# Subtractions of the first batch on VectorE, the first down-projection tile inside the up-projection, and fewer attention steps beside it

## The chip, the core and the metric

The kernel runs on one core of a Trainium2 chip. The metric is device microseconds of one execution; the time before is 673.47 us, the median of three runs (673.11 to 674.36).

## The reference, cut to what matters

Four batches of 576 positions go through windowed attention (8 heads of 64, window 64), a gated feed-forward layer, and a routed layer of eight experts.

```python
scores = scale * q @ k.T;  scores = where(0 <= rel < 64, scores, -1e9)
x = softmax(scores) @ v                                  # per batch and head, then heads side by side: 576 x 512
h = relu(x @ w_in)                                       # 512 -> 1024
conv_out = sum_k conv_w[k] * h shifted by k - 1          # three taps along the positions
y = (h * sigmoid(conv_out)) @ w_out                      # 1024 -> 512
e = argmax(y @ w_gate), held over from the position before where sigmoid(y @ w_local) >= 0.5
out = softmax(y @ w_gate)[e] * (relu(y @ w1[e]) @ w2[e])
```

## The kernel before, in words

**Numbers in two halves.** Matrix products run on float32 values split into a rounded high half H and a low half L, and each product is three: H times H, H times L, L times H. A split costs one ScalarE instruction (the rounding) and one subtraction. The feed-forward weights arrive as 64-bit floats and are first put together from two 32-bit words by three VectorE instructions (`bits64`, lines 558, 560, 562), then rounded by ScalarE and subtracted (`conv_chunk`, lines 583 and 584): `conv_in` does this for chunks of w_in (128 rows by 512 columns, eight in all), `conv_out` for the eight blocks of w_out. `conv_out` also transposes its block (line 602) and multiplies it with the gate weights (line 606), so that the routing logits come out of the down-projection as ten further columns.

**Stages.** The attention of batch 0 (`attention_first`) has nothing to run beside. It is written out by hand as the string `FIRST` of tokens, which sets the order of every engine there (the planner is off). After it, batch b's feed-forward part runs together with the attention of batch b+1: `mix` asks `main(b)` for one turn after the other (one turn per six accumulation steps) and, after each, takes as many of the 25 steps of `attention(b + 1)` as `share(b)` has allowed by then. In batch 0, 16 of the 25 steps are written beside the 32 turns of the up-projection and the rest beside the 16 turns of the four down-projection tiles. This program order gives the priorities; outside `FIRST` a planner puts each engine's instructions in order, and takes a later one first where an engine would otherwise stand still by its own reckoning. After batch 3 come the routing and the experts' tiles.

**The tokens of `FIRST`.** The digits are pair of heads (4 is the first pair of batch 1) and part. T: transposes of k, q and the tails on TensorE (lines 172 and 185), with k, q, t their evictions (q on ScalarE, line 196 for batch 1). S and R: scores on TensorE and their row maxima on VectorE (line 230). E: the exponentials (ScalarE, line 242, three of them). N and M: normalization on VectorE (N has lines 251 to 253 and the first product of line 255; M the other product). A and a: the probabilities transposed (line 270) and evicted by ScalarE. V, x, l: the product with v (line 298), its high half (ScalarE, line 305), its low half (VectorE, line 308). c, h, u: the three steps of a w_in chunk on VectorE, its rounding on ScalarE (line 650), its subtraction on GpSimd (line 652). D: matmuls of no use that keep TensorE busy (line 162). Z: a GpSimd memset and the loads of a pair of batch 1 on SP.

**Loads.** SP issues nearly all of them, in order. Before `FIRST`, pairs 0 to 3 of batch 0 and the first six chunks of w_in are asked for; the first two chunks stand between pairs, the other four in a row (line 571). The next pairs follow with Z0 and Z1.

**The up-projection** (`ffn`). For each of eight blocks f of 128 columns: two halves of twelve matmuls (line 432) into two banks, relu on ScalarE (line 439), the middle tap on ScalarE (451), two taps on VectorE (452, 453), tanh on ScalarE (454), the gate's product on VectorE (455), then gH by ScalarE (460) and gL (461) on GpSimd for all but the very last block. In batch 0 each block also starts one w_out block (and, for the first two, one of the last two w_in chunks), whose rounding, subtraction and transposes come one block later.

**The down-projection** (`ffn_out(i, fold)`). A tile of 128 positions takes 24 accumulation steps (eight blocks, three products each) into two banks at once (262 and 260 columns wide), so 48 matmuls (line 474), then two evictions and a store.

Of the kernel before, what the change touches and what calls it, by code (L numbers as in the profile page):

```python
# [21 lines left out]
def kernel(  # L22
# [70 lines left out]
    if True:  # L93
# [313 lines left out]
        def ffn(b):  # L407
            xs_b = xT.pop(b)
            fin = []
            t0 = b * S  # L410
            for f in range(KF):
                if b == B - 1 and f == 5:
                    gate(R0, I0)
                    gate_exp(0, I0)
                if b == 0:
                    if cin:
                        fin.append(conv_in(*cin.pop(0)))
                        if len(fin) > 1:
                            fin.pop(0)()
                    fin.append(conv_out(f))  # L420
                    if f:
                        fin.pop(0)()
                hbuf = hb[hcnt[0] % 2]
                hcnt[0] += 1
                for half in range(2):
                    ps = psm.tile([P, 512], F32, tag="m", name="psM")
                    c0 = half * HS
                    n = 0
                    for kk in range(KD):
                        xH, xL = xs_b[kk]  # L430
                        for wt, xt in ((winH, xH), (winH, xL), (winL, xH)):
                            nc.tensor.matmul(  # L432
                                ps[:, 0:HS], wt[:, kk, f * P:(f + 1) * P], xt[:, c0:c0 + HS],
                                start=n == 0, stop=n == 3 * KD - 1,
                            )
                            n += 1
                            if n == 6:
                                yield
                    nc.scalar.activation(hbuf[:, 1 + c0:1 + c0 + HS], ps[:, 0:HS], AF.Relu, scale=0.5)  # L439
                    yield  # L440
                t = tb[(b * KF + f) % 3]
                last = b == B - 1 and f == KF - 1
                cuts = (0, HS - 1, S) if last else (0, S)
                e1 = nc.vector if last else nc.gpsimd
                for u, w in zip(cuts, cuts[1:]):
                    tt = t[:, u:w]
                    h0, h1, h2 = (hbuf[:, j + u:j + w] for j in range(3))
                    if last:
                        nc.vector.tensor_scalar(tt, h1, cw[:, 1, f:f + 1], None, op0=ALU.mult)
                    else:  # L450
                        nc.scalar.activation(tt, h1, AF.Copy, scale=cw[:, 1, f:f + 1])
                    nc.vector.scalar_tensor_tensor(tt, h0, cw[:, 0, f:f + 1], tt, op0=ALU.mult, op1=ALU.add)  # L452
                    nc.vector.scalar_tensor_tensor(tt, h2, cw[:, 2, f:f + 1], tt, op0=ALU.mult, op1=ALU.add)
                    nc.scalar.activation(tt, tt, AF.Tanh)
                    nc.vector.scalar_tensor_tensor(tt, tt, 1.0, h1, op0=ALU.add, op1=ALU.mult)
                    done = u
                    while done < w:
                        r = (t0 + done) % RING
                        m = min(w - done, RING - r)
                        nc.scalar.activation(gH[:, f, r:r + m], t[:, done:done + m], AF.Copy)  # L460
                        e1.tensor_tensor(gL[:, f, r:r + m], t[:, done:done + m], gH[:, f, r:r + m].bitcast(F32), op=ALU.subtract)  # L461
                        done += m
            for x in fin:
                x()
# [122 lines left out]

        def conv_in(c, kk):
            fs = slice(c * CC, (c + 1) * CC)
            return conv_chunk(chunk_in(c, kk), winH[:, kk, fs], winL[:, kk, fs], nc.gpsimd, early.get((c, kk)))[1]  # L590

        def conv_out(kk):

            src = w_out.rearrange("(k p) f -> p k f", p=P)
            f, fin = conv_chunk(src[:, kk, :], woutH[:, kk, 0:DM], woutL[:, kk, 0:DM], nc.gpsimd)

            def finish():
                fin()
                wt = y_p.tile([P, KD, P], F32, tag="ysb", name="wt")
                pt = psa.tile([P, 512], F32, tag="a", name="psWT")  # L600
                for j in range(KD):
                    nc.tensor.transpose(pt[:, j * P:(j + 1) * P], f[:, j * P:(j + 1) * P], ident)
                nc.scalar.activation(wt.rearrange("p j f -> p (j f)"), pt, AF.Copy)
                ps = psa.tile([P, 512], F32, tag="a", name="psW")
                for j in range(KD):
                    nc.tensor.matmul(ps[:, 0:E1], wt[:, j, :], wgl[:, j, :], start=j == 0, stop=j == KD - 1)  # L606
                wH, wL = woutH[:, kk, DM:DW], woutL[:, kk, DM:DW]
                nc.scalar.activation(wH, ps[:, 0:E1], AF.Copy)
                nc.vector.tensor_tensor(wL, ps[:, 0:E1], wH.bitcast(F32), op=ALU.subtract)

            return finish
# [3 lines left out]
            S11 a00 R10 V00 R11 E10 A01 A02 S12 c00 x00 a01 l00 R12 a02 V01 c01 V02 x01 T20 x02 l01 E11 T21 l02 k2 T22  # L615
            t2 c02 q2 v2 E12 S20 S21 R20 N1 S22 E20 M1 A10 a10 R21 h0 V10 R22 A11 u0 x10 A12 a11 l10 Z0 T30 c10 a12
            V11 k3 E21 V12 c11 T31 T32 x11 t3 x12 l11 q3 l12 c12 E22 v3 S30 S31 R30 N2 S32 E30 M2 A20 a20 R31 h1 V20
            R32 A21 u1 x20 A22 a21 l20 T40 c20 a22 V21 k4 E31 V22 c21 T41 T42 x21 t4 x22 l21 q4 l22 c22 E32 c30 c31
            c32 h2 N3 h3 u2 M3 D9 A30 a30 u3 c40 V30 c41 A31 x30 A32 a31 l30 c42 a32 V31 c50 V32 x31 l31 x32 h4 l32
            c51 u4 c52 h5 u5 Z1  # L620
        """

        with tc.manual_schedule():
            warm(bank(0), 6)
            load_pair(0, 0)
            nc.vector.memset(wgl[:, :, E + 1:E1], 0.0)
            KC = 3 * KF
            taps = cv.tile([P, CC, 2], U32, tag="raw", name="cr", bufs=2)[0:KC, 0:P]
            nc.scalar.dma_start(out=taps.rearrange("r p t -> r (p t)"), in_=conv_w.rearrange("k (f x) -> (k f) x", f=KF))
            nc.scalar.dma_start(out=wgl[:, :, 0:E], in_=w_gate.rearrange("(k p) e -> p k e", p=P))  # L630
            nc.scalar.dma_start(out=wgl[:, :, E:E + 1], in_=w_local.rearrange("(k p) e -> p k e", p=P))
            cin = [(c, kk) for c in range(FF // CC) for kk in range(KD)]
            load_pair(0, 1)
            for i, (c, kk) in enumerate(cin[0:6]):
                early[c, kk] = load_chunk(st_p.tile([P, CC, 2], U32, name=f"raw{i}"), chunk_in(c, kk))
                if i < 2:
                    load_pair(0, 2 + i)
            part = {}

            def others(s_, i, g):  # L640

                c, kk = divmod(i, KD)
                fs = slice(c * CC, (c + 1) * CC)
                if s_ == "c":
                    if g == 0:
                        part[i] = cv.tile([P, CC], F32, name="lf")
                    bits64(early[c, kk], part[i], (g,))
                elif s_ == "h":
                    cin.pop(0)
                    nc.scalar.activation(winH[:, kk, fs], part[i], AF.Copy)  # L650
                elif s_ == "u":
                    nc.gpsimd.tensor_tensor(winL[:, kk, fs], part[i], winH[:, kk, fs].bitcast(F32), op=ALU.subtract)
                elif s_ == "w":
                    part["f"] = cv.tile([P, CC], F32, tag="lf", name="cf")[0:KC, 0:P]
                    bits64(taps, part["f"])
                elif s_ == "W":
                    part["ps"] = bank(0)
                    nc.tensor.transpose(part["ps"][:, 0:KC], part["f"], ident[0:KC, 0:KC])
                elif s_ == "Y":
                    nc.vector.tensor_copy(cw.rearrange("p k f -> p (k f)"), part["ps"][:, 0:KC])  # L660
                elif s_ == "D":
                    warm(bank(0), i)
                else:
                    nc.gpsimd.memset(qbds[i], 0.0)
                    load_pair(1, i)

            attention_first(FIRST, others)

# [243 lines left out]

        def share(b):

            n1, n2, na = 4 * KF, 4 * (4 + b % 2), 34 if b == 0 else 28
            return lambda m: 16 * m // n1 if m <= n1 else 16 + (na - 16) * (m - n1) // n2

        def main(b):
            yield from ffn(b)
            if b < B - 1:  # L920
                for i in range(b * S // P, (b + 1) * S // P):
                    yield from ffn_out(i, True)

        for b in range(B):
# [321 lines left out]
```

## Time and profile before

| | |
|---|---|
| median of three runs | 673.47 us |
| the profiled execution | 671.16 us |
| its span, first to last instruction | 669.4 us |
| TensorE busy, mean granted clock | 635.6 us (95%), 0.982 |
| VectorE busy | 500.5 us (75%) |
| ScalarE busy | 471.3 us (70%) |
| GpSimd busy | 151.5 us (23%) |

The profile is of one execution, so its parts add up to 671.16 and not to the median. Matmuls overlap in it, and their ends are modelled: a TensorE that is busy all the time can still be at half clock. The granted clock stands beside the busy time for that reason; 1.00 is 2.4 GHz and 0.50 is 1.2 GHz.

### The profile page before, as it was taken

To read this page: it belongs to the slowest core of one execution; us is meant where nothing else is said; L and a number is where in the kernel's file an instruction comes from. 1 tells how busy PE (TensorE), PEld (TensorE's weight loads), DVE (VectorE), ACT (ScalarE), POOL (GpSimd) and SP (SyncE) were. 2 spreads that over 40 slices of the span, in tenths; PEclk is the share of its full clock that TensorE was granted. 3 is DMA by queue.
4 is the path that set the end of the run, shared out by engine and by line. 5 is a ranking of instruction groups with operands and counts; after the bars stand their busy time and mean duration, and the time that the engine had idled before them with its cause. 6 is when DMAs were issued, how large, how long until landed. Compare 5 with 4: busy or idle time off the path is not lost.

```text
span 669.4 us, 12937 instructions
## 1 busy us (share of the span) xinstructions
PE 635.6 (95%) x4398; PEld 554.2 (83%) x4398; DVE 500.5 (75%) x989; ACT 471.3 (70%) x1003; POOL 151.5 (23%) x172
## 2 busy tenths in 40 slices
PE   6858898999999999999999999999999999999995
PEld 4647897899999999999978878888888888888884
DVE  4988987436884168725777788899899889889982
ACT  3855786536885478835625489888888988988982
POOL 2324625000330013303522221211211211211101
PEclk9989897899999999999999999999999999999998
DMA  8884414333234221108002147511451444512770
GB/s 166 214 214 108 130 46 117 77 95 95 64 69 104 64 52 33 32 33 315 1 0 79 48 174 256 194 48 52 153 164 64 145 157 157 166 41 71 240 273 14
DMA packets 91881, 75.77 MB, mean 113 GB/s; under 512 B 72266, under 2 KB 72290, under 8 KB 91812
## 3 DMA queue, kind: packets, MB, share of 16 engines
q1 hardware_dynamic: 85696, 63.78, 32.2%
q0 software_dynamic: 3680, 10.75, 4.8%
q10 hardware_dynamic: 2436, 0.37, 0.4%
q8 instruction: 36, 0.59, 0.4%
q14 instruction: 33, 0.27, 0.1%
HBM read 127.84 MB, written 11.27 MB: 208 GB/s over the span
## 4 chain that ended last, share of the span: by engine, by line
PE 41%; issue 32%; DMA 12%; DVE 6%; SPq 3%; POOL 2%; ACT 1%; ACTq 0%; POOLq 0%
PE psO L474 14%; PE psM L432 13%; DMA out_dram<-h,sidx 10%; PE psA L218 4%; PE psA L298 3%; PE psA L270 2%; PE psA L185 2%; POOL xg L1022 2%; PE psG L543 1%; DMA kt<-in_k_dram 1%; DVE lf L560 1%; PE psW L606 1%; DVE h L452 1%; PE psO L514 1%; SPq L141 1%
## 5 line engine op out<-in xcount | busy, mean ns | idle before, releaser
L432 PE MATMUL psM<-x,winH 128*128 128x288 f32 x512 | 111.0, 305 | 1.4 <-ACT h L439 1.3
L461 POOL TENSOR_TENSOR gL<-h,gH 128x576 fp32r<-128x576 f32 (+6 forms) x54 | 60.6, 1132 | 163.6 <-ACT gH L460 150.3
L432 PEld LDWEIGHTS psM<-x,winH 128*128 128x128 f32 x512 | 82.4, 189 | 3.7 <-ACT h L439 2.1
L1087 POOL DMA_INDIRECT out_dram<-h,sidx x23 | 23.3, 1014 | 233.4 <-ACT h L1086 233.4
L432 PE MATMUL psM<-x,winL 128*128 128x288 f32 x256 | 75.7, 296 | 0.0
L474 PE MATMUL psO<-woutH,gH 128*128 128x262 f32 (+2 forms) x240 | 68.8, 315 | 0.7 <-ACT gH L460 0.7
L474 PE MATMUL psO<-woutL,gH 128*128 128x262 f32 (+2 forms) x240 | 66.7, 306 | 1.2 <-POOL woutL L584 1.2
L1003 DVE TENSOR_TENSOR gL<-raw,gH 128x1024 fp32r<-128x1024 f32 x56 | 65.6, 1220 | 2.2 <-ACT gH L998 0.7
L474 PE MATMUL psO<-woutH,gL 128*128 128x262 f32 (+2 forms) x240 | 65.7, 304 | 0.0
L242 ACT ACTIVATE sS<-sS,mx 128x128 f32<-128x128 f32 (+1 forms) x144 | 55.2, 386 | 12.7 <-DVE mx L230 12.5
L1003 DVE TENSOR_TENSOR winL<-raw,winH 128x1024 fp32r<-128x1024 f32 x48 | 56.4, 1235 | 3.6 <-ACT winH L998 3.6
L998 ACT ACTIVATE gH<-raw 128x1024 fp32r<-128x1024 f32 x56 | 55.8, 1066 | 0.0
L1003 DVE TENSOR_TENSOR woutL<-raw,woutH 128x1024 fp32r<-128x1024 f32 x44 | 51.0, 1221 | 2.8 <-ACT woutH L998 2.8
L432 PEld LDWEIGHTS psM<-x,winL 128*128 128x128 f32 x256 | 48.2, 188 | 0.2
L998 ACT ACTIVATE winH<-raw 128x1024 fp32r<-128x1024 f32 x48 | 47.0, 1062 | 0.0
L1081 PE MATMUL psO<-x,hh 128*128 128x512 f32 x144 | 46.7, 404 | 0.0
L230 DVE CUSTOM_DVE_ANT_0 sS<-psA,mask 128x128 f32<-128x128 f32 (+1 forms) x135 | 31.0, 278 | 21.0 <-PE psA L218 16.8
L1003 DVE TENSOR_TENSOR x<-raw,x 128x1024 fp32r<-128x1024 f32 x36 | 42.0, 1220 | 5.2 <-ACT x L998 4.2
L474 PEld LDWEIGHTS psO<-woutL,gH 128*128 128x128 f32 x240 | 42.8, 190 | 3.2 <-POOL woutL L584 1.6
L474 PEld LDWEIGHTS psO<-woutH,gH 128*128 128x128 f32 x240 | 42.7, 190 | 2.7 <-ACT gH L460 0.9
L1081 PE MATMUL psO<-gH,hh 128*128 128x512 f32 x112 | 44.6, 398 | 0.0
L1081 PE MATMUL psO<-gH,hl 128*128 128x512 f32 x112 | 44.0, 393 | 0.0
(288 smaller groups left out, 1656.9 us busy)
## 6 DMA issues: line engine op xcount, KB each, us to landing
raw<-in_moe_w_dram SPq DMA_DIRECT2D x184, 512.0 KB
v<-in_v_dram SPq DMA_DIRECT2D x56, 128.0 KB
y_dram<-ysb SPq DMA_DIRECT2D x18, 256.0 KB
kt<-in_k_dram SPq DMA_DIRECT2D x32, 128.0 KB
raw<-in_moe_w_in_dram SPq DMA_DIRECT2D x8, 512.0 KB
raw<-in_moe_w_out_dram SPq DMA_DIRECT2D x8, 512.0 KB
qt<-in_q_dram SPq DMA_DIRECT2D x30, 128.0 KB
y_dram<-x SPq DMA_DIRECT2D x2, 256.0 KB
```

The source lines that it names most:

```text
L185: nc.tensor.transpose(ps[:, n * P:(n + 1) * P], src[:, n].rearrange("p h d -> p (h d)"), ident)
L218: nc.tensor.matmul(ps[:, j * P + lo:(j + 1) * P], qbd[:, c, :], kT[:, k0:W * (c + 1)], start=True, stop=True)
L230: nc.vector.tensor_tensor_reduce(sS[:, c, lo:P], ps[:, j * P + lo:(j + 1) * P], mask[:, lo:P], -scale, -NEG, op0=ALU.add, op1=ALU.min, acc ...
L242: nc.scalar.activation(sS[:, c, lo:P], sS[:, c, lo:P], AF.Exp, scale=-1.0, bias=mx[:, c:c + 1], accum_out=sume[:, c:c + 1],)
L298: nc.tensor.matmul(ps[64 * h:64 * h + 64, W * j:W * j + W], vt[:, h, :], a[0:kk, j, 64 * h:64 * h + 64], start=True, stop=True,)
L432: nc.tensor.matmul(ps[:, 0:HS], wt[:, kk, f * P:(f + 1) * P], xt[:, c0:c0 + HS], start=n == 0, stop=n == 3 * KD - 1,)
L461: e1.tensor_tensor(gL[:, f, r:r + m], t[:, done:done + m], gH[:, f, r:r + m].bitcast(F32), op=ALU.subtract)
L474: nc.tensor.matmul(p_[:, 0:cs.stop - cs.start], gt[:, kk, r:r + P], wt[:, kk, cs], start=n == 0, stop=n == 3 * KF - 1,)
L998: nc.scalar.activation(H_, raws[kk], AF.Copy)
L1003: nc.vector.tensor_tensor(L_, raws[kk], H_.bitcast(F32), op=ALU.subtract)
L1081: nc.tensor.matmul(ps, a[:, kk], w[:, kk % 2, :], start=n == 0, stop=n == 3 * KF - 1)
L1087: nc.gpsimd.indirect_dma_start(out=out[:, :], out_offset=bass.IndirectOffsetOnAxis(ap=sidx[:, t:t + 1].bitcast(U32), axis=0), in_=o, in_of ...
```

## The change

In batch 0 the subtractions of gL, of woutL and of the last two winL chunks are issued on VectorE instead of GpSimd. Tile 0 of the down-projection becomes a generator made before the loop (`out0`, a turn per three accumulation steps); from block 2 on, the first half of each block also takes one turn of it, so that six of its eight blocks are issued in the up-projection, two blocks behind. `share(0)` allows 12 steps of attention by the end of the up-projection and spreads the others, counted up to 29, over the 14 turns that are left. In `FIRST`, the last two pairs are put in another order: V21 and V22 ahead of T40, E31 behind x22, q4 behind E32, N3 and M3 ahead of chunk 3's first step (chunk 2 is then h2, chunk 3 h3), and D is 24 matmuls in three tokens instead of nine in one. Chunks 4 and 5 of w_in are loaded with Z0, behind the first pair of batch 1.

```diff
--- before.py
+++ after.py
@@ -437,11 +437,13 @@
                             if n == 6:
                                 yield
                     nc.scalar.activation(hbuf[:, 1 + c0:1 + c0 + HS], ps[:, 0:HS], AF.Relu, scale=0.5)
+                    if b == 0 and half == 0 and f > 1:
+                        next(out0)
                     yield
                 t = tb[(b * KF + f) % 3]
                 last = b == B - 1 and f == KF - 1
                 cuts = (0, HS - 1, S) if last else (0, S)
-                e1 = nc.vector if last else nc.gpsimd
+                e1 = nc.vector if last or b == 0 else nc.gpsimd
                 for u, w in zip(cuts, cuts[1:]):
                     tt = t[:, u:w]
                     h0, h1, h2 = (hbuf[:, j + u:j + w] for j in range(3))
@@ -587,12 +589,12 @@
 
         def conv_in(c, kk):
             fs = slice(c * CC, (c + 1) * CC)
-            return conv_chunk(chunk_in(c, kk), winH[:, kk, fs], winL[:, kk, fs], nc.gpsimd, early.get((c, kk)))[1]
+            return conv_chunk(chunk_in(c, kk), winH[:, kk, fs], winL[:, kk, fs], nc.vector, early.get((c, kk)))[1]
 
         def conv_out(kk):
 
             src = w_out.rearrange("(k p) f -> p k f", p=P)
-            f, fin = conv_chunk(src[:, kk, :], woutH[:, kk, 0:DM], woutL[:, kk, 0:DM], nc.gpsimd)
+            f, fin = conv_chunk(src[:, kk, :], woutH[:, kk, 0:DM], woutL[:, kk, 0:DM], nc.vector)
 
             def finish():
                 fin()
@@ -615,9 +617,9 @@
             S11 a00 R10 V00 R11 E10 A01 A02 S12 c00 x00 a01 l00 R12 a02 V01 c01 V02 x01 T20 x02 l01 E11 T21 l02 k2 T22
             t2 c02 q2 v2 E12 S20 S21 R20 N1 S22 E20 M1 A10 a10 R21 h0 V10 R22 A11 u0 x10 A12 a11 l10 Z0 T30 c10 a12
             V11 k3 E21 V12 c11 T31 T32 x11 t3 x12 l11 q3 l12 c12 E22 v3 S30 S31 R30 N2 S32 E30 M2 A20 a20 R31 h1 V20
-            R32 A21 u1 x20 A22 a21 l20 T40 c20 a22 V21 k4 E31 V22 c21 T41 T42 x21 t4 x22 l21 q4 l22 c22 E32 c30 c31
-            c32 h2 N3 h3 u2 M3 D9 A30 a30 u3 c40 V30 c41 A31 x30 A32 a31 l30 c42 a32 V31 c50 V32 x31 l31 x32 h4 l32
-            c51 u4 c52 h5 u5 Z1
+            R32 A21 u1 x20 A22 a21 l20 c20 a22 V21 c21 V22 x21 l21 x22 E31 T40 l22 T41 k4 T42 t4 E32 c22 q4 N3 h2 M3
+            D9 D9 D6 A30 a30 c30 u2 V30 c31 A31 x30 A32 a31 l30 c32 a32 V31 c40 V32 x31 l31 x32 h3 l32 c41 u3 c42 h4
+            c50 u4 c51 c52 h5 u5 Z1
         """
 
         with tc.manual_schedule():
@@ -631,8 +633,13 @@
             nc.scalar.dma_start(out=wgl[:, :, E:E + 1], in_=w_local.rearrange("(k p) e -> p k e", p=P))
             cin = [(c, kk) for c in range(FF // CC) for kk in range(KD)]
             load_pair(0, 1)
-            for i, (c, kk) in enumerate(cin[0:6]):
+
+            def stage_chunk(i):
+                c, kk = divmod(i, KD)
                 early[c, kk] = load_chunk(st_p.tile([P, CC, 2], U32, name=f"raw{i}"), chunk_in(c, kk))
+
+            for i in range(KD):
+                stage_chunk(i)
                 if i < 2:
                     load_pair(0, 2 + i)
             part = {}
@@ -663,6 +670,9 @@
                 else:
                     nc.gpsimd.memset(qbds[i], 0.0)
                     load_pair(1, i)
+                    if i == 0:
+                        stage_chunk(4)
+                        stage_chunk(5)
 
             attention_first(FIRST, others)
 
@@ -912,13 +922,20 @@
 
         def share(b):
 
-            n1, n2, na = 4 * KF, 4 * (4 + b % 2), 34 if b == 0 else 28
+            n1, n2, na = 4 * KF, 4 * (4 + b % 2), 28
+            if b == 0:
+                n2, na = 14, 29
+                return lambda m: 12 * m // n1 if m <= n1 else 12 + (na - 12) * (m - n1) // n2
             return lambda m: 16 * m // n1 if m <= n1 else 16 + (na - 16) * (m - n1) // n2
+
+        out0 = ffn_out(0, True, 3)
 
         def main(b):
             yield from ffn(b)
             if b < B - 1:
-                for i in range(b * S // P, (b + 1) * S // P):
+                if b == 0:
+                    yield from out0
+                for i in range(b * S // P + (b == 0), (b + 1) * S // P):
                     yield from ffn_out(i, True)
 
         for b in range(B):
```

## Rows read from the trace of the kernel before

**Rows 1.** Busy time by stretch: PE, PEld, DVE, ACT, POOL (instructions), PE clock, DMA.

```profile
45.00:51.00 6.00, 5.08 (x36) 3.72 (x36) 4.14 (x9) 2.18 (x6) 0.40 (x1) 0.50 0.98 257
51.00:105.00 54.00, 48.31 (x386) 45.87 (x386) 48.96 (x106) 38.72 (x103) 26.78 (x17) 0.96 0.38 106
105.00:130.00 25.00, 22.07 (x158) 19.57 (x158) 14.08 (x51) 14.43 (x48) 6.04 (x5) 0.80 0.31 80
130.00:370.00 240.00, 239.75 (x2062) 223.12 (x2061) 144.31 (x441) 144.84 (x427) 56.56 (x78) 1.00 0.26 73
```

**Rows 2.** The chain that ended last, 28 to 60 us: start, duration, what.

```profile
30.18 6.89 DMA kt<-in_k_dram
...
43.05 1.17 DVE sume L251
```

**Rows 3.** Timeline of ScalarE, 32 to 83 us.

```profile
39.37 1.19 ACT L196 ACTIVATE qbd<-psA 64x512 f32<-64x512 f32 x2 [0.31 <-PE psA L185]
40.59 0.40 ACT L242 ACTIVATE sS<-sS,mx 128x128 f32<-128x128 f32 x1
```

**Rows 4.** Timeline of TensorE, 24 to 85 us: start, duration, idle before.

```profile
39.22 1.15 PE L162 MATMUL psA<-ident 128*128 128x256 bf16 x9
...
45.50 0.42 PE L268 MATMUL psM<-ident,sS 128*64 128x128 f32 x1 [5.14 <-DVE sS L253]
...
50.35 0.85 PE L432 MATMUL psM<-x,winH 128*128 128x288 f32 x2
```

**Rows 5.** Timeline of SP's DMA queue: start and duration of issuing.

```profile
26.60 3.04 SPq L571 DMA_DIRECT2D raw<-in_moe_w_in_dram  x4
```

**Rows 6.** Groups of VectorE by line and shape, 60 to 112 us: busy us, mean ns.

```profile
L453 DVE SCALAR_TENSOR_TENSOR h<-h,cw 128x576 f32<-128x576 f32 x8 | 8.8, 1097 | 0.0
L452 DVE SCALAR_TENSOR_TENSOR h<-h,cw 128x576 f32<-128x576 f32 x8 | 8.5, 1067 | 0.0
L455 DVE SCALAR_TENSOR_TENSOR h<-h 128x576 f32<-128x576 f32 x8 | 6.8, 850 | 0.0
L560 DVE SCALAR_TENSOR_TENSOR lf<-raw,lf 128x512 uint32<-128x512 uint32 x8 | 6.6, 819 | 0.1
...
L558 DVE TENSOR_SCALAR lf<-raw 128x512 uint32<-128x512 uint32 x8 | 4.6, 572 | 0.0
```

**Rows 7.** Timeline of VectorE, 85 to 89 us, where GpSimd has nothing.

```profile
85.29 0.42 DVE L558 TENSOR_SCALAR lf<-raw 128x512 uint32<-128x512 uint32 x1
...
86.36 0.68 DVE L560 SCALAR_TENSOR_TENSOR lf<-raw,lf 128x512 uint32<-128x512 uint32 x1
86.96 0.81 DVE L453 SCALAR_TENSOR_TENSOR h<-h,cw 128x576 f32<-128x576 f32 x1
...
88.96 0.75 DVE L455 SCALAR_TENSOR_TENSOR h<-h 128x576 f32<-128x576 f32 x1
```

**Rows 8.** The page's costliest groups: a subtraction on VectorE in the experts' stage.

```profile
L1003 DVE TENSOR_TENSOR woutL<-raw,woutH 128x1024 fp32r<-128x1024 f32 x44 | 51.0, 1221 | 2.8 <-ACT woutH L998 2.8
```

**Rows 9.** Groups of GpSimd by line and shape, 50 to 130 us.

```profile
L461 POOL TENSOR_TENSOR gL<-h,gH 128x576 fp32r<-128x576 f32 x8 | 13.8, 1725 | 13.3 <-ACT gH L460 10.1 <-ACT woutH L608 3.2
L584 POOL TENSOR_TENSOR woutL<-lf,woutH 128x512 fp32r<-128x512 f32 x8 | 12.0, 1498 | 18.6 <-ACT woutH L583 18.6
```

**Rows 10.** Groups of VectorE by line and shape, 130 to 350 us: attention's pieces.

```profile
L230 DVE CUSTOM_DVE_ANT_0 sS<-psA,mask 128x128 f32<-128x128 f32 x70 | 16.8, 287 | 12.0 <-PE psA L218 11.7
L255 DVE TENSOR_TENSOR sS<-sS,sume 128x1024 f32<-128x1024 f32 x9 | 10.9, 1216 | 0.0
L308 DVE TENSOR_TENSOR x<-psA,x 128x192 fp32r<-128x192 f32 x30 | 10.3, 345 | 20.2 <-ACT x L305 20.0
```

**Rows 11.** TensorE, 50 to 130 us: a group of line 474, and a wait (us, times, longest).

```profile
L474 PE MATMUL psO<-woutH,gL 128*128 128x262 f32 x8 | 2.4, 302 | 0.0
...
PE psO L474 <- POOL woutL L584: 1.2, 2, 0.7
```

**Rows 12.** Groups of ScalarE by line and shape, 50 to 130 us: the rounding.

```profile
L583 ACT ACTIVATE woutH<-lf 128x512 fp32r<-128x512 f32 x8 | 5.0, 628 | 1.8 <-DVE lf L562 1.7
```

## Prediction

> **What bounds the kernel now.** I read the stretches first. From 130 to 370 us TensorE has 239.75 busy us of 240 at a granted clock of 1.00 [rows 1]: nothing that happens on another engine there can take much off. Earlier there is room. A busy us at clock 0.50 (1.2 of 2.4 GHz) does the work of half a us, so I multiply busy time by clock: 2.5 of 6 us in 45 to 51, 46.4 of 54 in 51 to 105, 17.7 of 25 in 105 to 130. So 3.5, 7.6 and 7.3 us are lost there. Because TensorE is full afterwards, what is won before 130 should arrive at the end nearly one for one, and that is my rule for the sum.
>
> Next I read the end of the first attention. The chain of waits goes through the load of the first keys of batch 1: kt lands at 37.07 (30.18 + 6.89) [rows 2]. T40 transposes it, and everything behind T40 in TensorE's order (V21, V22, T41) stands late. ScalarE then has q4 (39.37, two pieces, 1.19 us) ahead of E32, whose first exponential begins at 40.59 [rows 3]. VectorE finishes chunk 3 and only then normalizes: the first instruction of N3 (line 251) takes 1.17 us of the chain from 43.05 [rows 2]. TensorE meanwhile idles 5.14 us before A30 at 45.50 and starts the up-projection at 50.35 [rows 4], most of this at half clock [rows 1].
>
> Then the up-projection. VectorE has 48.96 busy us of 54 there [rows 1], the highest share beside TensorE, and part of it is not work: where GpSimd subtracts at the same time, VectorE's rows are long. That sets the pace.
>
> **The change, part by part.**
>
> *Order of the last two pairs.* V21, V22 go ahead of T40; E31 goes behind x22; q4 goes behind E32; N3 and M3 go ahead of chunks 3, 4 and 5. Without q4 in front and without waiting for kt, E32 should begin near 39.0 (x22 near 37.8, then three exponentials of some 0.4 each), end near 40.2, and N3 follow: VectorE holds only chunk 2's last step before it. N3 up to the first product is about 0.2 + 0.25 + 0.25 + 0.35 us (estimates from its chain steps without GpSimd beside it), so A30 can start near 41.3 instead of 45.50: 4.2 us. Chunk 3's subtraction (u2 now) comes later on GpSimd, so it no longer stands beside N3. The way from A30 to the up-projection, 4.85 us [rows 4] at clock 0.50, should shrink by about 0.9 where TensorE is still at the upper level. Against this, the fourth chunk, which the first matmuls of the up-projection need, is now converted behind N3 and M3; I take off 0.5. Sum: **-4.6 us**. Ends: -6 (all of A30's wait goes) and -2 (kt or the late chunks hold it).
>
> *Chunks 4 and 5 loaded later.* SP issued chunks 2 to 5 in one run of 3.04 us from 26.60 [rows 5], ahead of batch 1's first pair. Two of the four now go behind all ten DMAs of that pair: kt is issued some 1.5 us earlier and shares the DMA engines with 1 MB less. Chunk 4 is wanted by VectorE near 45, some 7 us after its issue; batch 1's second pair goes 1.5 us later and is wanted near 70. Cost nothing; if chunk 4 landed late, only c40 and what follows waits, 1 to 2 us on VectorE. The GpSimd memset in the same token does not move.
>
> *15 more matmuls of D.* Nine took 1.15 us [rows 4], so 24 take about 3.1 us, 15 of them 1.9. They stand between T42 (near 38.6) and A30 (near 41.3), where TensorE would wait for N3: hidden. Without that cover they cost up to 1.9, or 3.8 at half clock. What they should buy is a granted clock of 1.00 at A30; that is in the 0.9 above.
>
> *18 subtractions from GpSimd to VectorE* (8 gL of 576 columns, 8 woutL and 2 winL of 512; the six winL of the first attention stay on GpSimd). Taken away: the stretching. In 60 to 112 the means are 1.097 (line 453), 1.067 (452), 0.850 (455), 0.819 (560), 0.572 (558), eight each [rows 6]; with GpSimd idle the same shapes take 0.81, 0.81, 0.75, 0.68, 0.42 [rows 7]. Eight times the differences: 2.3 + 2.1 + 0.8 + 1.1 + 1.2 = 7.5 us. Added: line 1003 subtracts 1024 columns on VectorE in 1.221 us [rows 8], so 0.69 for 576 and 0.61 for 512: 8 x 0.69 + 10 x 0.61 = 11.6 us. Net **+4.1** on VectorE, and each is now queued: what stands behind a gL on VectorE (the next taps, the next maxima) waits if ScalarE has not yet written gH.
>
> The row shows 16 GpSimd spans of 13.8 + 12.0 = 25.8 us [rows 9] stretching VectorE by only 7.5. The Trainium skill, "SBUF — State Buffer", section Who interferes with whom, says that a VectorE instruction with two SBUF inputs and a GpSimd instruction that reads SBUF exclude each other for the whole instruction, whichever came first. By that rule the relief could be up to the whole 25.8; the measured 7.5 is what I use, since nothing that VectorE did not lose can come back.
>
> *Four attention steps (13 to 16 of 25) go into the down-projection.* VectorE's part of them: three maxima at 0.287, one product over 1024 columns at 1.216, three subtractions at 0.345 [rows 10], together 3.1 us (small pieces left out). They leave the stretch where VectorE is full and come where it has 14.08 busy of 25 [rows 1]. **-3.1 us.** Their TensorE work only moves. The load of batch 2's first pair, which hangs on step 16, is issued later on SP; it is wanted a whole down-projection later. With na = 29 all 25 steps are out by the 43rd of 46 turns, so three turns of six accumulation steps cover the last subtraction.
>
> *Tile 0 written into the up-projection.* The planner does this already: all eight products of gL with the wide half of woutH for tile 0 are there before 130, and no ninth [rows 11]. The lag of two blocks makes sure that gL and woutL are there; TensorE's wait for woutL from GpSimd was 1.2 us in all [rows 11]. I count it under the next point.
>
> *The stretch 105 to 130.* It loses 7.3 us, most of it clock. With fewer VectorE steps ahead of the last blocks, and without GpSimd's hop in gL and woutL, gaps should be fewer. Nothing in the trace prices it; ends are -5.5 (three quarters won) and +2 (13 steps are too dense for their chains). I take a quarter: **-1.8 us**.
>
> **Sum.** -4.6 + 4.1 - 3.1 - 1.8 = -5.4 us. The profiled execution took 671.16, so 665.8 there; the median of the runs is 2.3 above it, 673.47, so **668.1**.
>
> **Rivals.**
> 1. *VectorE waits for ScalarE.* Each of the 18 needs the rounded copy that ScalarE has just been asked for; such a copy takes 0.628 [rows 12]. If VectorE meets every one unfinished, it stands still 18 x 0.63 = 11.3 us in its fullest stretch: -5.4 + 11.3 = +5.9, 679.4. It decides from 9 of the 18 on. For it: VectorE runs its queue in order and is full there. Against it: the planner orders by when operands should be ready and has conversions to put between. The Trainium skill, "Perfetto Trace Analysis", section Optimizing Scalar/DVE Operations, says that work of a saturated VectorE may be worth giving to GpSimd; that speaks against this change, and the row of VectorE's fullness agrees with its condition.
> 2. *The lock costs more than the rows show.* If the stretching also delays what follows, since taps, rounding and subtraction hang on each other, taking GpSimd out could give back half of the 14.9 us lost in 51 to 130: -4.6 - 7.5 = -12.1, 661.4. This is the skill's lock rule as a mechanism of this kernel. For it: 25.8 us of GpSimd spans stand within the chain of a block. Against it: VectorE's added 11.6 us.
> 3. *Nothing arrives.* The up-projection starts earlier, waits for chunks 3 to 7 and w_out's, which still pass through one VectorE with 1 us more to do, and ends when it did: 673.5. For it: VectorE's fullness. Against it: VectorE, too, starts its normalization, and so its conversions, sooner.
>
> **How the numbers follow.** Forecast 0.60, rival 1 0.17, rival 2 0.14, rival 3 0.09. A measurement of this kernel tells about 0.2%, 1.3 us. Faster: forecast and rival 2, 0.74; same 0.09; slower 0.17. The forecast's bounds, with the start at -6 or -2, VectorE at -2 or +4 and the last stretch at -5.5 or +2, give at best -13.5 and at worst +4; the range goes from 660.0 to 677.0 and so takes in rival 2, rival 3 and the milder half of rival 1.
>
> **What would show it.** Right: A30 at 41 to 42 instead of 45.50, granted clock near 1.00 from there, the first matmul of line 432 near 45.5 to 46.5; lines 452 and 453 at 0.81 mean; gL on VectorE near 0.69; no GpSimd span in the first batch after the last winL of line 652. Wrong: waits of VectorE's gL or woutL for ScalarE of several us in total; the last block's gL not earlier than 112; a clock of 0.5 somewhere in 105 to 130 again; or TensorE idle after 130, which would break the rule that early gains arrive.

## The result, and the profile after

The changed kernel takes 666.03 us (median of five runs, 664.43 to 667.32) against 673.47 before: a ratio of 0.9888, with a 95% interval of 0.9863 to 0.9913. The forecast was 668.1, the range 660.0 to 677.0. The profiled execution took 664.43 us, with a span of 662.7 us, against 671.16 and 669.4.

First the stretches of [rows 1], after the change (same columns: TensorE, weight loads, VectorE, ScalarE, GpSimd busy, granted clock, DMA).

```profile
45.00:51.00 6.00, 4.22 (x36) 3.47 (x36) 4.38 (x14) 3.66 (x13) 2.12 (x2) 1.00 0.80 197
51.00:105.00 54.00, 47.30 (x371) 44.36 (x370) 52.57 (x121) 39.66 (x100) 3.34 (x3) 0.97 0.49 132
105.00:130.00 25.00, 23.34 (x190) 21.82 (x189) 11.50 (x53) 13.32 (x48) 0.00 (x0) 0.87 0.24 57
130.00:370.00 240.00, 239.33 (x2061) 222.12 (x2060) 149.27 (x440) 143.23 (x424) 56.83 (x79) 1.00 0.26 73
```

From 130 us TensorE is as full as before. In 51 to 105 it is no better off: 54 - 47.30 x 0.97 = 8.1 us lost, where it was 7.6. Between 105 and 130 it loses 25 - 23.34 x 0.87 = 4.7 instead of 7.3. The half clock of 45 to 51 is gone, but in 105 to 130 it came again, as in these 2.5 us (same columns):

```profile
105.50:108.00 2.50, 2.50 (x14) 2.46 (x14) 2.50 (x6) 0.69 (x4) 0.00 (x0) 0.50 0.01 3
```

Next TensorE's timeline where the first attention ends, which answers to [rows 4].

```profile
40.05 0.82 PE L162 MATMUL psA<-ident 128*128 128x256 bf16 x6
40.71 0.27 PE L268 MATMUL psO<-ident,sS 128*64 128x128 f32 x1
...
43.07 0.51 PE L432 MATMUL psM<-x,winH 128*128 128x288 f32 x2
```

A30 (line 268) starts at 40.71 instead of 45.50, right behind the last of the matmuls of no use (line 162) and without a wait. The up-projection starts at 43.07 instead of 50.35.

On ScalarE (timeline, as [rows 3]) the order is as written: E32, whose first exponential this is, stands before q4, which begins at 39.60.

```profile
38.45 0.39 ACT L242 ACTIVATE sS<-sS,mx 128x128 f32<-128x128 f32 x1
```

VectorE's groups in 51 to 105 us, against [rows 6] and [rows 8]. The line numbers have moved by two: 454, 455, 457 and 560 are 452, 453, 455 and 558 of before; 463 is gL, 586 the weights' subtraction.

```profile
L455 DVE SCALAR_TENSOR_TENSOR h<-h,cw 128x576 f32<-128x576 f32 x8 | 6.5, 809 | 0.0
...
L457 DVE SCALAR_TENSOR_TENSOR h<-h 128x576 f32<-128x576 f32 x8 | 6.0, 749 | 0.0
L463 DVE TENSOR_TENSOR gL<-h,gH 128x576 fp32r<-128x576 f32 x7 | 5.2, 740 | 0.0
L586 DVE TENSOR_TENSOR woutL<-lf,woutH 128x512 fp32r<-128x512 f32 x6 | 4.1, 683 | 0.2 <-ACT woutH L585 0.2
L560 DVE TENSOR_SCALAR lf<-raw 128x512 uint32<-128x512 uint32 x9 | 3.8, 417 | 1.1 <-DMA raw<-in_moe_w_in_dram 1.1
```

The taps are back at 0.81 (line 454 has 0.807), the gate at 0.75, the first step of a chunk at 0.42: the durations that [rows 7] have where GpSimd is idle. A subtraction takes 0.74 and 0.68 (my 0.69 and 0.61), and VectorE hardly ever stands before one: 0.2 us for the weights, nothing for gL.

**Two numbers for a kernel.** The difference lies ahead of 130 us, so I use one window for each kernel: 100 us from its first matmul of line 432. What TensorE loses there is 100 less busy time multiplied by granted clock. It has two parts: idle time, and busy time at the lower clock.

```profile
50.35:150.35 100.00, 91.38 (x751) 85.01 (x750) 69.85 (x184) 62.54 (x182) 32.83 (x21) 0.93 0.35 95
```

That was the kernel before; the changed one is this.

```profile
43.07:143.07 100.00, 89.87 (x741) 83.73 (x739) 75.14 (x207) 63.50 (x183) 5.45 (x4) 0.95 0.45 118
```

Before: 100 - 91.38 x 0.93 = 15.0 lost (8.6 idle, 6.4 by the clock), and 669.4 - 50.35 = 619.0 us from the first matmul to the end. After: 14.6 lost (10.1 and 4.5) and 619.6 to the end. The difference between the two, some 604 to 605, is the work that remains for TensorE. So this profile's gain of 6.7 us is the earlier start (7.3), and what is lost afterwards is the same. Is that one effect, or several that cancel?

### The profile page after: what moved, and what is told of

Same layout as the page of the kernel before. It is cut to its first block, busy times and chain, and to the rows that moved or that the text cites. A ratio compares the mean times of both kernels' runs of the same rounds, so it can differ in the third digit from the quotient of the medians.

```text
span 662.7 us, 12963 instructions
## 1 busy us (share of the span) xinstructions
PE 632.9 (96%) x4413; PEld 552.2 (83%) x4413; DVE 502.9 (76%) x1007; ACT 469.9 (71%) x1003; POOL 121.3 (18%) x154
## 4 chain that ended last, share of the span: by engine, by line
PE 42%; issue 31%; DMA 14%; DVE 9%; ACT 2%; POOL 1%; POOLq 0%; DVEq 0%; ACTq 0%
PE psO L476 14%; PE psM L432 13%; DMA out_dram<-h,sidx 12%; PE psA L218 3%; PE psA L298 3%; PE psA L270 2%; PE psA L185 1%; DVE lf L562 1%; DVE lf L564 1%; PE psG L545 1%; DVE sS L230 1%; DVE lf L560 1%; PE psA L221 1%; PE psO L516 1%; ACT sS L242 1%
## 5 line engine op out<-in xcount | busy, mean ns | idle before, releaser
L432 PE MATMUL psM<-x,winH 128*128 128x288 f32 x512 | 110.6, 304 | 5.1 <-ACT h L439 5.1
L432 PEld LDWEIGHTS psM<-x,winH 128*128 128x128 f32 x512 | 82.1, 189 | 7.2 <-ACT h L439 6.2
L463 POOL TENSOR_TENSOR gL<-h,gH 128x64 fp32r<-128x64 f32 (+5 forms) x46 | 45.7, 1001 | 211.8 <-ACT gH L462 203.7
L432 PE MATMUL psM<-x,winL 128*128 128x288 f32 x256 | 75.7, 297 | 0.8 <-POOL winL L659 0.8
L476 PE MATMUL psO<-woutL,gH 128*128 128x262 f32 (+2 forms) x240 | 65.2, 306 | 0.0
L242 ACT ACTIVATE sS<-sS,mx 128x128 f32<-128x128 f32 (+1 forms) x144 | 55.1, 387 | 11.3 <-DVE mx L230 11.2
L432 PEld LDWEIGHTS psM<-x,winL 128*128 128x128 f32 x256 | 48.0, 188 | 1.2 <-POOL winL L659 1.0
L1098 PE MATMUL psO<-gL,hh 128*128 128x512 f32 x112 | 43.7, 390 | 0.0
```

Of the source, the lines that this page charges most:

```text
L242: nc.scalar.activation(sS[:, c, lo:P], sS[:, c, lo:P], AF.Exp, scale=-1.0, bias=mx[:, c:c + 1], accum_out=sume[:, c:c + 1],)
L432: nc.tensor.matmul(ps[:, 0:HS], wt[:, kk, f * P:(f + 1) * P], xt[:, c0:c0 + HS], start=n == 0, stop=n == 3 * KD - 1,)
L476: nc.tensor.matmul(p_[:, 0:cs.stop - cs.start], gt[:, kk, r:r + P], wt[:, kk, cs], start=n == 0, stop=n == 3 * KF - 1,)
L1098: nc.tensor.matmul(ps, a[:, kk], w[:, kk % 2, :], start=n == 0, stop=n == 3 * KF - 1)
```

## The experiments

**Eight kernels from three parts.** A is the order of the first attention with its 24 matmuls of D and the later loads; V the 18 subtractions on VectorE; M tile 0 in the up-projection with the new shares. The diffs are those of the change, part by part. V by itself, for one:

```diff
-                e1 = nc.vector if last else nc.gpsimd
+                e1 = nc.vector if last or b == 0 else nc.gpsimd
...
-            return conv_chunk(chunk_in(c, kk), winH[:, kk, fs], winL[:, kk, fs], nc.gpsimd, early.get((c, kk)))[1]
+            return conv_chunk(chunk_in(c, kk), winH[:, kk, fs], winL[:, kk, fs], nc.vector, early.get((c, kk)))[1]
...
-            f, fin = conv_chunk(src[:, kk, :], woutH[:, kk, 0:DM], woutL[:, kk, 0:DM], nc.gpsimd)
+            f, fin = conv_chunk(src[:, kk, :], woutH[:, kk, 0:DM], woutL[:, kk, 0:DM], nc.vector)
```

A alone. 

> The kernel before with only the new order of the first attention (with 24 matmuls of D) and the later loads of chunks 4 and 5. Parts add up (my sum): first matmul of the up-projection some 5 to 7 us earlier than 50.35, and 4 to 5 us off the time, about 669. Rival, the first attention is hidden by VectorE's queue in the up-projection: the matmul starts as early, and the time stays within 1.5 us of the kernel before.

V alone. 

> The kernel before with only the 18 subtractions of the first batch on VectorE. My sum: VectorE gets 4.1 us more to do, less something for a shorter chain, so between -2 and +4 us against the kernel before. Rival, the port: GpSimd's spans delay whole chains, and this part alone takes 4 us or more off.

M alone. 

> The kernel before with only tile 0 written into the up-projection and the new share of attention steps. My sum: 3.1 us of VectorE's work leave the full stretch, so 1 to 4 us off. Rival, the planner does most of this already: within 1.5 us of the kernel before.

A and V. 

> The changed kernel without its third part (tile 0 and the shares are as before). If parts add up: the changed kernel plus 1 to 4 us, so 667 to 670. If the third part does nothing: 666. If VectorE is overfull without it: 671 or more.

A and M. 

> The changed kernel with the 18 subtractions of the first batch on GpSimd again. My sum (VectorE gets 1 to 4 us more by them): no slower than the changed kernel, 663 to 667. Rival, the port: GpSimd's spans stretch VectorE's instructions again and delay whole chains, 670 or more, with lines of the taps at 1.0 to 1.1 us mean instead of 0.81.

V and M. 

> The changed kernel with the first attention's order and loads as before. If parts add up: 4 to 5 us slower than the changed kernel, about 670.5. If VectorE's queue hides the first attention: 666 to 667.

Measured, each against runs of the kernel before on the same chip (medians 672.96 and 673.24). "Lost" and "to the end" are worked out as above, from each one's profile.

| kernel | median us | ratio, 95% interval | first L432 | to the end | lost |
|---|---|---|---|---|---|
| before | 673.47 | 1 | 50.35 | 619.0 | 15.0 |
| A | 669.22 | 0.9933 (0.9908 to 0.9959) | 44.06 | 623.8 | 19.8 |
| V | 666.60 | 0.9901 (0.9878 to 0.9924) | 53.42 | 612.9 | 8.9 |
| M | 674.08 | 1.0015 (0.9999 to 1.0032) | 52.92 | 618.9 | 14.7 |
| A, V | 664.64 | 0.9892 (0.9865 to 0.9920) | 44.51 | 617.8 | 12.9 |
| A, M | 670.04 | 0.9957 (0.9940 to 0.9974) | 42.57 | 622.5 | 17.9 |
| V, M | 666.52 | 0.9915 (0.9890 to 0.9939) | 50.70 | 613.7 | 10.5 |
| A, V, M | 666.03 | 0.9888 (0.9863 to 0.9913) | 43.07 | 619.6 | 14.6 |

"To the end" less "lost" is 603 to 605 in every line, so the account holds. A profile is one run: in starts and losses it can differ from the medians by a few us. What follows:

- V is worth most: 1.0% without A (V against before, V and M against M), 0.4 to 0.7% with A. In the profiles TensorE loses 3.3 to 6.9 us less with V in each of the four pairs. The start does not show it: it is 3.1 later with V alone and 2.2 earlier with V beside M.
- A is worth 0.7% alone and 0.6% beside M, but 0.1 and 0.3% beside V, which is within the intervals. It brings the first matmul forward in every profile and gives some of it back: the loss is 3 to 5 us higher with A in each of the four pairs.
- M shows nothing: +1.0 us alone, with an interval (0.9999 to 1.0032) that takes in no change, and the other pairs lie between -0.04% and +0.24%.

So the start's 7.3 us and a loss that did not move are two effects: what A adds to the loss stands against what V takes off it. Of the expectations, A's sum held in start and time. V's did not (-2 to +4, measured -6.7); its rival had the number. With A and M the time was 670.04 where my sum said 663 to 667, again the rival's number, though only one tap was long (1.18, the other 0.80). V and M together gave the 666 to 667 of the rival, and A and V came nearest to the third part doing nothing. That the planner does M's work already fits the times of M.

The windows that carry this, first A alone, then V alone.

```profile
44.06:144.06 100.00, 88.18 (x710) 81.27 (x708) 77.88 (x189) 63.56 (x182) 32.55 (x22) 0.91 0.42 110
```

```profile
53.42:153.42 100.00, 93.88 (x804) 87.40 (x803) 75.32 (x223) 67.44 (x205) 3.85 (x3) 0.97 0.37 100
```

V puts VectorE's busy time up, from 69.85 to 75.32, and TensorE still loses 6 us less: 2.5 of them are idle time (8.6 to 6.1) and 3.6 the clock (6.4 to 2.8). VectorE's amount of work was not what TensorE waited for. The waits of ScalarE show one place where the chain of a block was late. In the kernel before (us, times, longest; 50 to 130 us):

```profile
ACT h L454 <- DVE h L453: 7.3, 6, 2.1
```

The tanh stood 7.3 us in all before the second tap; with V alone this wait is 0.7. That it is what delayed TensorE is not shown.

**GpSimd busy, but on nobody's way.** V can have gained in two ways. One is the port, as the expectations call it: VectorE's instructions are long while GpSimd reads beside them. The other is GpSimd's slower result on the way to gL and woutL. This kernel has V and puts the port's load back.

```diff
                         nc.scalar.activation(gH[:, f, r:r + m], t[:, done:done + m], AF.Copy)
                         e1.tensor_tensor(gL[:, f, r:r + m], t[:, done:done + m], gH[:, f, r:r + m].bitcast(F32), op=ALU.subtract)
+                        if b == 0:
+                            for _ in range(2):
+                                nc.gpsimd.tensor_tensor(t, t, gH[:, f, r:r + m].bitcast(F32), op=ALU.subtract)
```

> The kernel before with the 18 subtractions on VectorE (as in the run with that part alone, 666.6), and beside them 16 subtractions of no use on GpSimd, two per block of the first batch, in place on the block's t when it is done with, so that nobody waits for them. GpSimd is as busy as in the kernel before, and its results are on nobody's way. If the port is what cost (VectorE's instructions stretched, and what hangs on them late): taps back at 1.0 us mean and more, and 672 to 680. If GpSimd's own time on the way to gL and woutL is what cost: 665 to 668.

Measured: 684.12 us, ratio 1.0148 (1.0122 to 1.0174), 17.5 us above V alone (the kernel before, run beside each, has 673.40 here and 672.96 there). Its window, groups of GpSimd (51 to 130 us) and of VectorE (51 to 120 us), and TensorE's longest wait (50 to 140 us; 0.9 in all with V alone):

```profile
52.49:152.49 100.00, 87.82 (x639) 80.79 (x638) 84.18 (x195) 59.35 (x173) 30.24 (x19) 0.83 0.29 81
```

```profile
L464 POOL TENSOR_TENSOR h<-h,gH 128x576 f32<-128x576 f32 x16 | 26.4, 1648 | 41.9 <-DVE gL L461 23.5 <-PE psA L185 9.3 <-DVE woutL L612 5.0
```

```profile
L455 DVE SCALAR_TENSOR_TENSOR h<-h 128x576 f32<-128x576 f32 x7 | 7.4, 1062 | 0.0
...
L587 DVE TENSOR_TENSOR woutL<-lf,woutH 128x512 fp32r<-128x512 f32 x5 | 6.8, 1359 | 0.0
```

```profile
PE psO L477 <- DVE woutL L587: 6.4, 4, 2.9
```

26.4 us of useless GpSimd time raise VectorE's busy time by 84.18 - 75.32 = 8.9 us and TensorE's loss from 8.9 to 27.1. The 8.9 is too low for the stretching, since this window holds 195 of VectorE's instructions and the other 223: line by line, in 51 to 130 us, the taps, gates, woutL and steps of chunks are some 14 us longer than with V alone (my sum from the groups). Of what TensorE loses more, only 6.1 of 18.2 us are idle time (12.2 against 6.1); 12.1 are the clock (14.9 against 2.8), which fell after gaps: TensorE has nothing in 80.0 to 82.5 us, and the granted clock is 0.50 from there to 87.5. This pair of kernels is a clean one: no engine is seen to wait for GpSimd's useless results, and the timelines have the instructions of TensorE, ScalarE and VectorE in the same order as with V alone, but for three accumulator reads of VectorE that one trace lacks. So GpSimd's load costs time without being on anybody's way. The time lies above the 672 to 680 of the first expectation, and the place is another: it is less the taps (0.90 and 0.81) than the gate and woutL that are long. This kernel has both loads at once, the subtractions and the stretching, which may be why it is worse than the kernel before.

**gL alone on VectorE.** Only the first line of V's diff.

> The kernel before with only the eight gL on VectorE; the weights' ten subtractions stay on GpSimd. If the effect goes by GpSimd's time taken away (13.8 of 29 us): about half of the 6.4 us, so 669 to 671. If it comes from gL's place behind gH in the block's chain: 666 to 668. If it comes from woutL, for which TensorE waits: 672 to 674.

Measured: 667.85 us, 0.9914 (0.9889 to 0.9940), the upper end of the second expectation, which was gL's place in the chain and not the port. gL alone does most of what V does; the difference to V lies within the intervals. Its window, and two of VectorE's groups (51 to 120 us):

```profile
51.42:151.42 100.00, 92.48 (x797) 86.41 (x796) 74.75 (x212) 66.69 (x202) 18.39 (x13) 0.97 0.37 100
```

```profile
L453 DVE SCALAR_TENSOR_TENSOR h<-h,cw 128x576 f32<-128x576 f32 x8 | 8.3, 1036 | 0.0
L461 DVE TENSOR_TENSOR gL<-h,gH 128x576 fp32r<-128x576 f32 x8 | 8.3, 1033 | 0.1
```

TensorE loses 10.3 (7.5 idle, 2.8 by the clock), but the stretching has not gone: the taps have 1.04 and 0.94, the gate 0.88, gL 1.03. Above 0.81, 0.75 and 0.75 that is 6.2 us, where taps and gate had 5.2 in [rows 6]. So most of V's gain came in a kernel that still has long taps. M alone speaks the same way: within its interval it is as fast as the kernel before, though the second step of a chunk takes 1.27 in 60 to 112 us, where [rows 6] has 0.82:

```profile
L562 DVE SCALAR_TENSOR_TENSOR lf<-raw,lf 128x512 uint32<-128x512 uint32 x9 | 11.4, 1269 | 0.1
```

The port's load can cost much, as the run before shows; that its absence is what V gained by is not shown. The other explanation is not shown either: in the kernel before, no engine is seen to wait for gL, and TensorE waits 1.2 us for woutL [rows 11]. And in these kernels the planner has put the engines in other orders than before, which no run separates from the rest. The cause of V's gain stays open.

**Nine matmuls of D.** In `FIRST`, `D9` for `D9 D9 D6`.

> The changed kernel with nine matmuls of D instead of 24. My account: the 15 stood where TensorE waited for N3 and gave it a granted clock of 1.00 at A30; without them TensorE idles about 2 us before A30, and the clock falls to 0.5 around 41 to 47 or it does not: if it falls, 1 to 3 us slower, if not, within 1 us. Rival: they stand in the way, and it gets 1 us faster.

Measured: 662.80 us, 0.9841 (0.9809 to 0.9873), 3.2 us below the changed kernel; the two intervals overlap a little. Its first matmul is later, 44.68, and it loses 11.3 instead of 14.6. TensorE idles 1.05 us before A30, and the clock is at 1.00 in 41 to 47. The rival named the sign, but not the way: it is not A30 that gets earlier (41.16). The planned order of the up-projection is another one here.

**One matmul less.** `D9 D9 D5`.

> The changed kernel with 23 matmuls of D instead of 24: 0.1 us of work that is in nobody's way, but the planner writes another order of the up-projection for it. If orders are worth the same: within 1 us of the changed kernel. If the planner's order is worth some us by itself: off by 2 us or more, either way, and then what nine matmuls instead of 24 won is no effect of the 15.

Measured: 665.91 us, 0.9883 (0.9856 to 0.9909), as the changed kernel. But the expectation was wrong about the order: in the two timelines TensorE, VectorE and ScalarE run the same sequence of instructions, so the planner wrote no other one. The run shows that the same order gives the same time twice; what another order is worth it does not test, and it leaves open what the nine matmuls won by.

**No subtraction on GpSimd before batch 1.** The changed kernel with

```diff
-                    nc.gpsimd.tensor_tensor(winL[:, kk, fs], part[i], winH[:, kk, fs].bitcast(F32), op=ALU.subtract)
+                    nc.vector.tensor_tensor(winL[:, kk, fs], part[i], winH[:, kk, fs].bitcast(F32), op=ALU.subtract)
```

> The changed kernel with the six winL subtractions of the first attention on VectorE too, so that GpSimd subtracts nothing before batch 1. Four VectorE instructions there are stretched by 0.6 to 1.1 us each, 3.7 in all, and six subtractions would add 6 x 0.61 = 3.7. The port as a matter of VectorE's time only: within 1 us of the changed kernel. The port as a delay of chains: 1 to 3 us faster.

Measured: 661.43 us, 0.9820 (0.9789 to 0.9851), 4.6 us below the changed kernel and better than either expectation. It has the lowest median of the study, though its interval overlaps that of nine matmuls. One of VectorE's groups in 42 to 55 us, first of the changed kernel, then of this one:

```profile
L564 DVE SCALAR_TENSOR_TENSOR lf<-raw,lf 128x512 uint32<-128x512 uint32 x3 | 3.5, 1179 | 0.0
```

```profile
L564 DVE SCALAR_TENSOR_TENSOR lf<-raw,lf 128x512 uint32<-128x512 uint32 x3 | 2.0, 682 | 0.0
```

The other two steps of a chunk fall from 0.96 to 0.68 and from 0.69 to 0.42. The planned order differs here too, so how much of the 4.6 us is the stretching is not shown.

**Both of these.** Nine matmuls and the winL subtractions on VectorE.

> The changed kernel with the six winL subtractions of the first attention on VectorE too, and nine matmuls of D: the two that each beat it, together. If they add up: 657 to 659. If both are one and the same gain (less lost before the up-projection's first blocks) or orders of the planner: 661 to 663.

Measured: 665.07 us, 0.9856 (0.9828 to 0.9884). This is slower than both expectations; the two don't add up. With all subtractions on VectorE nine matmuls are no better than 24 (3.6 us worse by the medians, but the intervals overlap), where they were 3.2 us better without. Its profile starts the up-projection at 44.68 and loses 18.6. So the 3.2 us can't be called an effect of the 15 matmuls alone. Of these four kernels all but the one with 23 matmuls have planned orders of their own; whether that sets which one is faster was not shown.

## Why the prediction was right or wrong

The time was right to 2 us, and the direction, but with luck in it: the terms that made it up were in part wrong and cancelled. My sum was -5.4 us. By themselves A, V and M measure -4.5, -6.7 and +1.0, -10.2 together, and the changed kernel has -7.5.

- *What is won before 130 us arrives.* Right: time to the end less loss is 603 to 605 us in all eight.
- *Order of the last two pairs, -4.6.* The mechanism held: E32 began at 38.45 (forecast 39.0), A30 at 40.71 (41.3), the first matmul at 43.07, earlier than the 45.5 that I named. A alone measures -4.5 (0.9933), but not in the way of the sum: in its profile the start is 6.3 us earlier and 4.8 us are lost again (1.5 us net in these two executions, less than the medians show). I took off 0.5 for the late conversions; both parts of the term were too small. Beside V it is worth 0.1 to 0.3%.
- *Loads of chunks 4 and 5, nothing.* Not tried by themselves. VectorE waits 1.1 us for a chunk of w_in in 51 to 105.
- *15 more matmuls, hidden.* Hidden from A30 to within 0.3 us: its operand was ready at 40.44 (line 253, 40.19 + 0.25), A30 began at 40.71. That they pay was not shown: with nine the clock stayed at 1.00 behind A30 too, and that kernel was not slower.
- *18 subtractions, +4.1 on VectorE.* This is the step that failed. VectorE's busy time rose, by 5.5 us in V alone, so the sum in it was nearly right. To take it as a sum in the time was wrong: I had VectorE's fullness set the pace of the up-projection, and V alone gives -6.7 us (0.9901). An us of VectorE's time has no fixed price here: some 14 us of stretching by useless subtractions on GpSimd cost 17.5 us in the same order of instructions, and 5.5 us more by V came with 6.7 us less. What V won by stays open: gL alone on VectorE wins 5.8 us (0.9914) with long taps.
- *Four attention steps later, -3.1.* Wrong: M gives nothing where it was to give 1 to 4 us, beside V too, where GpSimd has only 3.8 us in the window to lengthen anything. I counted VectorE's work in a stretch that it did not bound. That the planner had tile 0 in the up-projection already was right.
- *105 to 130 us, -1.8.* It became -2.6 in the profile (7.3 to 4.7), within the ends. But the clock of 0.5 in 105 to 130, which I had named as a sign of being wrong, came again, and the stretch holds later work than before, since all begins 7.3 us earlier.
- *Rival 1, VectorE waits for ScalarE:* fell. It waited 0.3 us in all before the 18 subtractions (43 to 135 us).
- *Rival 2, the lock costs more than the rows show:* that stretching can cost its full length and more is shown by the run with useless subtractions (some 14 us and 17.5). That it cost the kernel before 7.5 us is not: V alone gives 6.7, a near number, but most of it comes with gL alone and long taps. It did not come on top of A, whose own loss stood against it. The Trainium skill, "SBUF — State Buffer", section Who interferes with whom, has the exclusion itself, and the rows of before, after and the run with useless subtractions agree (0.81 against 1.1, 0.68 against 1.36).
- *Rival 3, nothing arrives:* part of it is A's lost 4.8 us.
- *The range.* Its upper end should be 673.47 + 4 = 677.5, not 677.0; nothing hangs on it.

The Trainium skill's advice for a saturated VectorE ("Perfetto Trace Analysis", section Optimizing Scalar/DVE Operations) is bounded by its own next sentence, that GpSimd shares a port with VectorE. These runs agree with that sentence: VectorE was 91% busy in 51 to 105 us (48.96 of 54), and the kernel got 1.0% faster by giving it the work (V alone).

## What to carry to other kernels

Where TensorE is full later on, split a kernel's time into the moment at which its main work starts and what it loses afterwards: two parts that look alike in the time can then be told apart. An engine's busy share does not price a change: here VectorE got 5.5 us more to do and the kernel 6.7 us shorter. Where GpSimd and VectorE both read the on-chip memory, try all of the work on VectorE before balancing it. Where a planner orders the instructions, compare the orders of two profiles before a difference of a few us is given to one edit.

## What was not expected of the hardware

Subtractions on GpSimd that nobody waits for are not free: 26.4 us of them made a kernel 17.5 us (2.6%) slower than it was without them, with the same order on the other engines, and two thirds of what TensorE lost by them was its granted clock. And the start of the up-projection differed between profiles by up to 3.1 us (50.35 to 53.42) in kernels whose first attention is the same, so one profile's start says less than the runs' medians.
